# Delta rule and feed-forward on one core: where chunk 1's keys are turned, where w_in's third quarter waits, and how VectorE's background work is listed

## The chip, the cores and the metric

The kernel runs on one core of a Trainium2 chip. The metric is the device time of one execution in microseconds (us). A core has five engines that run beside each other, each in its own order: TensorE (PE; its weight loads are PEld), VectorE (DVE), ScalarE (ACT), GpSimd (POOL) and SyncE (SP), which here only issues DMAs. ScalarE and GpSimd issue some DMAs too. The clock that TensorE is granted changes during a run and is part of the profile.

## The reference

There are 4 batches of 8 heads, 768 positions of width 48. For each head a state matrix is carried along the sequence, and its output goes through a feed-forward block:

```python
k_n = k / (np.linalg.norm(k, axis=-1, keepdims=True) + 1e-06)
for t in range(S):
    y[:, :, t] = einsum('bhd,bhde->bhe', q[:, :, t], state)
    v_old = einsum('bhde,bhd->bhe', state, k_n[:, :, t])
    state = state + beta[t] * outer(k_n[:, :, t], v[:, :, t] - v_old)
x = y.transpose(0, 2, 1, 3).reshape(3072, 384)
h = x @ w_in            # 384 x 2048
out = (h / (1 + exp(-1.702 * h))) @ w_out     # 2048 x 384
```

w_in and w_out come in double precision (two 32-bit words an element), and the kernel turns them into 32-bit floats itself.

## The kernel before

**Units and steps.** The sequence is cut into 6 chunks of 128 positions; a unit is one chunk of one batch with its 8 heads, so there are 24 units, numbered chunk by chunk (units 0 to 3 are chunk 0, 4 to 7 chunk 1). Within a chunk the recurrence becomes a triangular system with the keys' products (gram, line 357, kept as G). It is solved in 4 blocks of 32 rows: `solve` multiplies by the inverse of a diagonal block (psU, copied by ScalarE to US), `below` multiplies the result by the rows underneath (psR), and `rest` subtracts this from V on VectorE. `scores` turns the queries (psT, QS) and makes the masked query-key products (psQ, M, with an affine_select on POOL); `queries`, `outputs` and `state` make psY, copy it to xT and add the new state to ST.

**Inverses.** `invert` (line 427) inverts all diagonal blocks of a chunk (or of two batches) on VectorE: NT holds the blocks, one head and block in a partition, YB the inverse. It is a chain of 25 products P, each with a sum. The blocks reach NT through DRAM (Nd), and the inverses come back through DRAM (Yd) as XB. For chunk 0 `diagonal` (line 411) makes the 32x32 blocks alone on TensorE (psD), copied to TW by VectorE and ScalarE. For all later units `prepare` (line 384) turns the keys (`turn`, psT copied to kT), makes the whole gram, sends all of G to DRAM and reads the blocks from there.

**Raw weights.** `conversion` (line 201) turns raw double words into floats with five VectorE instructions and a ScalarE Relu between them, through a scratch place in TW. w_in is converted in 8 pieces of 3x256 columns (two for each quarter), then w_out in 14 pieces (12 of one row block of 384, two of two). The raw words of w_in lie in the place of w_out, which has room for two quarters: quarters 0 and 1 are fetched at the start, 2 when 0 is converted, 3 when 1 is. w_out's raw words follow by a table, `fetches`: a transfer is issued when a given piece is done. `fill(n)` (line 289) issues the next n conversion instructions, and the program calls it at places written by hand.

**Order of the head.** All engines keep the order in which the program issues (`pinned`), and so does SP's queue of DMAs. The order is: chunk 0's keys are normalised and turned, its blocks made and inverted (`invert(0)`, interleaved with the first scores); then two pairs of units, 0 and 1, then 2 and 3, are solved in 8 hops each (`hops`, line 1031: a hop solves a block for one unit and multiplies below for the other). In the first pair each hop is followed by 4 filler products (`warm(NU)`, ps_warm) and `fill(1)`. After it come the loads of keys 7 and 8, the first raw words of w_out and queries. In the second pair each hop is followed by `fill(2)`, by a half `feed` of the first feed-forward product from hop 3 on, and by the work of `keys()` (line 1044): normalising unit 4 to 7's keys (ScalarE square, VectorE sum, POOL power, VectorE product), turning them, making G and sending the blocks round. `hidden` (line 678) makes the product ph and the activation gT; a half is 3 matmuls, a whole `hidden` 16 halves.

After the pairs the rest of w_in is converted, then `invert(1)` runs, one instruction pair for each of 25 halves of `feed`, and then 10 more conversion instructions (`fill(10)`).

**Woven steps.** From there `woven(n, share)` (line 921) runs for n from 3 to 24. Each step carries the three units n-1, n, n+1, normalises and prepares the keys of unit n+5, and takes `share` us of feed-forward work from a queue by the costs that the work yields (1.3 for a half). The queue begins with `both_written` (line 823), the second product (po) of the first feed-forward block, which goes through w_out's row blocks in the order of conversion and issues conversions (`fill(3)`, and more while the block isn't done) ahead of each; then `written`. Together they fill steps 3 to 6 (share 10.4). From step 7 on (share 19.5) the rest of the feed-forward blocks follow, with one product fewer of each eight (`seven`, for which POOL makes the combinations T1 to T4, L711).

Most instructions go through one helper and so have line 109 in the profile; tiles tell them apart.

Of the kernel before, what the change touches and what calls it, by code (L numbers as in the profile page):

```python
# [18 lines left out]
def kernel(  # L19
# [147 lines left out]

    def quarter(i):
        size = KC * NQ * 2
        return as_raw(raws[:, i % 2 * size : (i % 2 + 1) * size], (KC, NQ))  # L170

    def fetch_in(i, other=None):

        f = slice(i * NQ, (i + 1) * NQ)
        dst = as_rows(quarter(i))
        for j in range(KC):
            for p, r, m, step in x_rows:
                (other if other and p >= DP else sync)(
                    out=dst[p : p + m, j], in_=moe_w_in[r + j * step : r + j * step + m, f]
                )  # L180
# [18 lines left out]
    turns = [0]  # L199

    def conversion(dst, raw, shape):
# [12 lines left out]
        yield  # L214
        turns[0] ^= 1
        at = 3072 + turns[0] * 768
        t = TW[:, at : at + shape[0] * shape[1]].bitcast(I32).rearrange("p (j n) -> p j n", j=shape[0])
        f = t.bitcast(F32)
        ts(t, hi, E1 - 1, E1, op0=AND, op1=OR)
        yield  # L220
        stt(out=f, in0=lo.bitcast(U32), scalar=2.0**-32, in1=t, op0=ALU.mult, op1=ALU.add)
        yield
        stt(out=p, in0=hi, scalar=-(1 << 31), in1=p, op0=AND, op1=OR)
        yield
        stt(out=dst, in0=f, scalar=2.0**-20, in1=dst, op0=ALU.mult, op1=ALU.mult)
        yield

    def pieces():

        for i in range(4):  # L230
            for e in range(2):
                at = i * NQ + e * NPC
                raw = quarter(i)[:, :, e * NPC : (e + 1) * NPC, :]
                yield w_in[:, :, at : at + NPC], raw, (KC, NPC), ("in", 2 * i + e)
# [14 lines left out]
    def conversions():  # L249
# [3 lines left out]
        def begin(i):  # L253
            dst, raw, shape, name = whole[i]
            ops = conversion(dst, places[name[1]] if raw is None else raw, shape)
            next(ops)
            return ops

        after = begin(0)
        yield  # L260
        for i in range(len(whole)):
            ops = after
            next(ops)
            yield
            next(ops)
            yield
            if i + 1 < len(whole):
                after = begin(i + 1)
                yield
            next(ops)  # L270
            yield
            next(ops)
            done.add(whole[i][3])
            fetches.pop(whole[i][3], lambda: None)()
            yield

    fetches = {
        ("in", 1): lambda: fetch_in(2),
        ("in", 3): lambda: fetch_in(3),
        ("in", 5): lambda: fetch_out(3),  # L280
        ("in", 7): lambda: (fetch_out(4), fetch_out(5), fetch_out(6), fetch_out(7)),
# [5 lines left out]
    converting = conversions()  # L287

    def fill(n):
        for _ in range(n):  # L290
            next(converting, None)

    ready = {}
    inverse = {}

# [53 lines left out]

    def transposed(src, dst):  # L350
# [29 lines left out]
    def turn(n):  # L380
        kTs[n] = wk.tile([128, NP, 128], F32, tag="kT", name="kT", bufs=5)
        transposed(KN[n % len(KN)], kTs[n])
# [28 lines left out]
    def diagonal(b, D_):  # L411

        kT = kTs[b]
        ps = [ps_seq.tile([128, NP, 128], F32, tag="seq", name="psD") for _ in range(2)]
# [6 lines left out]
        for e in range(2):  # L421
            for blk in range(NB):
                u = slice(blk * BS, (blk + 1) * BS)
                copy = vec.tensor_copy if e == 0 or blk == 0 else act.copy
                copy(D_[u, e::2, :], ps[e][u, :, u])

    def invert(c, b0=0, nb=B):
# [7 lines left out]
        yield 0.0  # L435
# [20 lines left out]
        for i in range(1, HS):  # L456
# [6 lines left out]
            yield 0.0  # L463
# [3 lines left out]
        act.activation(X1, halves(Y)[1].rearrange("p l i -> p i l"), ACT.Copy)  # L467
        A = N[:, 0:HS, 0:HS]
        N10, Y0 = N[:, HS:, 0:HS], halves(Y)[0]
        for j, Q in ((0, 2), (2, 2), (4, 4), (8, 4), (12, 4)):  # L470
# [7 lines left out]
            yield 0.0  # L478
        for i, Q in ((0, 4), (4, 4), (8, 4), (12, 2), (14, 2)):
# [7 lines left out]
            yield 0.0  # L487
# [21 lines left out]
        yield 0.0  # L509
# [7 lines left out]
    class Step:  # L517
# [114 lines left out]
        def state(self, psS=None):  # L632
# [3 lines left out]
            for h in range(H):  # L636
# [4 lines left out]
                )  # L641
            St = ST[:, self.b, 0 : NP * D].rearrange("p (j d) -> p j d", j=NP)
            vec.tensor_tensor(St, psS, St, op=ALU.add)

        def outputs(self, state=False):
# [5 lines left out]
            if state:  # L651
                self.state(self.psS)
# [20 lines left out]

    def g_tile():

        return wk.tile([128, FQ, NTH], F32, tag="gT", name="gT", bufs=GB)
# [146 lines left out]
    def both_written(c, gT):  # L823

        po = [ps_moe.tile([128, DM], F32, tag="moe", name="po") for _ in range(HB)]
        for n, f in enumerate(order):
            while ("out", f - f % 2 if 4 <= f < 8 else f) not in done:
                fill(1)
            fill(3)
# [151 lines left out]
    for i in range(B, len(KN)):  # L981
        pool.memset(KN[i][:, :, D:DP], 0.0)

# [13 lines left out]
    for b in range(B):  # L997
# [3 lines left out]
        )  # L1001
    for b in range(B):
        load(b, ((QP, q),), sync)
    for b in range(B):
        load_values(b, sync)
    fetch_in(1, other_queue)
    for n in range(B, len(KN)):
        load(n, ((KN, k),), sync)
    for blk in range(NB):
        sync(out=bI[blk::NB, 1:], in_=betas[:, 1:, blk, :])  # L1010
    fill(6)
    for b in range(B):
        gram(b)
        warm(NA)
    late_U = spare("U")[:, 0 : H * D + XR]
    pair = [new_step(n) for n in range(B)]
    inverting = invert(0)
    for n in range(B):
        next(pair[n].scored)
        warm(NA)  # L1020
        run(pair[n].scored)
        warm(NA)
        if n == 0:
            ahead_of(inverting, 18)
    run(inverting)
    pool.memset(late_U[:, H * D :], 0.0)
    for s in pair:
        s.select()
    fill(5)
# [9 lines left out]
    def put_out(s):  # L1039
        s.queries()  # L1040
        s.outputs(True)
        steps.pop(s.n)

    def keys():

        def unit(n):
            yield from normalize_mixed(n)
            yield from prepare(n)

        work = [unit(n) for n in range(B, 2 * B)]  # L1050
        for t in range(18):
            for u in range(B):
                s = t - 3 * u
                if s >= 0 and s % 2 == 0:
                    next(work[u], None)
            yield
        for w in work:
            run(w)

    path = hops(*pair[:2])  # L1060
    for i in range(2 * NB):
        together(*next(path))
        warm(NU)
        fill(1)
    for s in pair[:2]:
        put_out(s)
        fill(1)
    load(7, ((KN, k),), sync)
# [16 lines left out]
    preparing = keys()  # L1085
    for i in range(2 * NB):
        together(*next(path))
        if i > 2:
            feed()
        fill(2)  # L1090
        ahead_of(preparing, 2 if i else 0)
    for s in pair[2:]:
        put_out(s)
        feed()
        fill(2)
        ahead_of(preparing, 2)
# [4 lines left out]
    while not ("in", 7) in done:  # L1101
        fill(1)
    run(preparing)
    inverting = invert(1)
    first = new_step(B)
    for i in range(25):
        ahead_of(inverting, 1)
# [5 lines left out]
    run(inverting)  # L1113
    while ffn:
        feed()
    fill(10)
# [35 lines left out]
```

## Time and profile before

| what | us |
|---|---|
| median of 3 runs (812.78 to 814.7) | 812.81 |
| the profiled execution, whole | 808.59 |
| its span in the profile | 806.6 |
| busy in the span: PE, DVE | 745.0, 499.7 |
| busy in the span: ACT, POOL | 238.6, 251.3 |
| mean granted TensorE clock | 0.951 |

The profile is of one execution, and its rows are timed from the start of its span. A group or timeline row names the engine, the line, the operation, the tile written and the tiles read (out<-in), the shape and the number; a bracket gives the engine's idle time before the row and what ended it. A matmul of 32-bit floats stands as two records. The window rows give busy time of each engine in a stretch, the granted clock (1.00 is full) and the share of the 16 DMA engines. The chain of work that ended last lists, in order of time, the pieces that the end waited for.

### The profile page before, as it was taken

The numbers are of one execution on the slowest core, as the hardware profiler recorded it, in microseconds if no ns is written. First come the engines' busy times: TensorE is split into PE (matmuls) and PEld (weight loads), VectorE is DVE, ScalarE is ACT, GpSimd is POOL, SyncE is SP. The second block draws the span as 40 slices with busy tenths as digits, with TensorE's granted clock in tenths as the row PEclk, the third lists the DMA queues.
The fourth block names the chain that finished last, engine by engine and source line by source line (L and its number), as shares of the span: only waits on it lengthen the run. The fifth ranks groups of instructions, "written<-read, shape, count | busy, mean of one in ns | idle before, by whom it ended". The sixth has DMA issues, their size and how long they took to land.

```text
span 806.6 us, 19689 instructions
## 1 busy us (share of the span) xinstructions
PE 745.0 (92%) x8464; PEld 633.7 (79%) x8464; DVE 499.7 (62%) x1029; ACT 238.6 (30%) x523; POOL 251.3 (31%) x222
## 2 busy tenths in 40 slices
PE   8678779777788899999999999999999999999998
PEld 6566668654455689889898898898898898988988
DVE  5798571898688767767677777786686671110000
ACT  3332353223322332232232332322322312312020
POOL 5002030011126735244262272272260320502213
PEclk9576799889999999999999999999999999999999
DMA  9946366344212420421422223214204011000000
GB/s 164 143 69 118 93 172 167 55 108 106 82 55 51 104 53 21 105 54 34 91 54 69 57 64 93 59 28 104 63 12 103 13 25 39 2 26 2 25 1 20
DMA packets 143655, 54.45 MB, mean 68 GB/s; under 512 B 113665, under 2 KB 138369, under 8 KB 143569
## 3 DMA queue, kind: packets, MB, share of 16 engines
q1 hardware_dynamic: 141936, 48.42, 27.2%
q0 software_dynamic: 1536, 4.52, 2.3%
q8 instruction: 66, 1.08, 0.6%
q10 hardware_dynamic: 96, 0.26, 0.1%
q14 instruction: 21, 0.16, 0.1%
HBM read 33.13 MB, written 18.87 MB: 64 GB/s over the span
## 4 chain that ended last, share of the span: by engine, by line
PE 67%; DVE 15%; issue 5%; DMA 5%; POOL 4%; SPq 2%; ACT 1%; DVEq 0%; POOLq 0%
PE ph L109 25%; PE po L109 23%; PE psY L109 5%; PE psU L109 5%; DVE P L109 4%; PE psQ L109 3%; DVE YB L109 3%; SPq L109 2%; DVE TW L109 2%; PE psR L109 2%; PE psT L109 2%; DVE w_out L109 2%; POOL TW L711 2%; DVE NT L109 1%; PE psG L109 1%
## 5 line engine op out<-in xcount | busy, mean ns | idle before, releaser
L109 PE MATMUL ph<-xT,w_in 128*128 128x256 f32 x1152 | 267.4, 389 | 0.0
L109 PEld LDWEIGHTS ph<-xT,w_in 128*128 128x128 f32 x1152 | 219.0, 194 | 33.0 <-DVE V L109 1.4
L109 PE MATMUL po<-w_out,gT 128*128 128x192 f32 (+1 forms) x736 | 150.3, 357 | 18.5 <-DVE w_out L109 10.8
L109 PEld LDWEIGHTS po<-w_out,gT 128*128 128x128 f32 x736 | 121.3, 191 | 36.6 <-DVE w_out L109 14.8
L711 POOL TENSOR_TENSOR gT<-gT 128x512 f32<-128x512 f32 x80 | 105.9, 1332 | 125.6 <-ACT gT L109 115.0
L109 DVE TENSOR_TENSOR V<-V,psR 64x384 f32<-64x384 f32 (+1 forms) x96 | 53.3, 556 | 130.5 <-PE psR L109 129.3
L109 DVE TENSOR_TENSOR P<-NT,YB 64x2 f32<-64x2 f32 (+9 forms) x200 | 97.3, 486 | 6.4
L109 ACT ACTIVATE gT<-ph 128x512 f32<-128x512 f32 x92 | 54.8, 596 | 152.9 <-PE ph L109 152.8
L109 PEld LDWEIGHTS psU<-V,XB 32*32 32x32 f32 x1536 | 61.7, 110 | 31.3 <-issue 15.4
L109 DVE TENSOR_REDUCE YB<-P 64x2 f32<-64x2 f32 (+9 forms) x200 | 81.7, 409 | 6.9
L109 PE MATMUL po<-TW,gT 128*128 128x192 f32 x480 | 83.0, 328 | 0.0
L109 ACT COPY US<-psU 32x384 f32<-32x384 f32 x92 | 43.2, 469 | 125.0 <-PE psR L109 115.1
L109 PE MATMUL psU<-V,XB 32*32 32x48 f32 x1536 | 73.2, 209 | 6.2 <-DVE V L109 5.3
L109 PEld LDWEIGHTS po<-TW,gT 128*128 128x128 f32 x480 | 77.9, 190 | 1.1 <-issue 0.3
L109 PE MATMUL psR<-US,G 32*32 32x48 f32 x2208 | 64.0, 208 | 0.8 <-ACT US L109 0.5
L578 POOL TENSOR_SCALAR_AFFINE_SELECT M<-M 128x1024 f32<-128x1024 f32 x19 | 23.7, 1245 | 120.0 <-DVE M L109 62.1
L109 DVE TENSOR_TENSOR o<-o,po 128x192 f32<-128x192 f32 x40 | 13.5, 351 | 75.8 <-PE po L109 75.3
L109 PEld LDWEIGHTS psR<-US,G 32*32 32x32 f32 x2208 | 54.2, 109 | 2.4 <-ACT US L109 1.1
L109 DVE TENSOR_TENSOR P<-NT 64x512 f32<-64x512 f32 (+7 forms) x50 | 44.5, 890 | 2.1
L94 POOL DMA_DIRECT2D KN<-in_k_dram x15 | 14.4, 960 | 93.5 <-PE psY L109 93.5
L109 PE MATMUL ps_warm<-ident 128*128 128x256 bf16 x176 | 31.6, 340 | 11.5 <-ACT G L109 6.5
L109 PE MATMUL psQ<-QS,kT 48*128 48x176 f32 (+1 forms) x368 | 35.6, 337 | 4.8 <-ACT QS L109 4.7
(110 smaller groups left out, 773.9 us busy)
## 6 DMA issues: line engine op xcount, KB each, us to landing
Nd<-G SPq DMA_DIRECT2D x20, 512.0 KB, 3.5
V<-in_v_dram SPq DMA_DIRECT2D x24, 192.0 KB, 3.1
out_dram<-o SPq DMA_DIRECT2D x24, 192.0 KB, 2.5
QP<-in_q_dram SPq DMA_DIRECT2D x22, 192.0 KB, 3.3
w_out<-in_moe_w_in_dram SPq DMA_DIRECT2D x18, 192.0 KB, 5.1
raw<-in_moe_w_out_dram SPq DMA_DIRECT2D x9, 384.0 KB, 5.3
NT<-Nd SPq DMA_DIRECT2D x24, 128.0 KB, 2.8
XB<-Yd SPq DMA_DIRECT2D x24, 128.0 KB, 3.1
```

Source lines behind the costliest of these rows:

```text
L94: dma(out=place(dst, n)[:, :, 0:D], in_=src[b, :, c * C : (c + 1) * C, :].rearrange("h p d -> p h d"),)
L109: return lambda *a, **kw: tc.keep_in_program_order(op(*a, **kw))
L578: (pool if self.n < B else nc.gpsimd).affine_select(out=self.M, in_=self.M, compare_op=ALU.is_gt, fill=0.0, base=0, pattern=[[0, H], [1, 1 ...
L711: (engine or nc.gpsimd).tensor_tensor(o, a, b, op=op)
```

## The change

Seven things change, all ahead of or inside the woven steps 3 and 4.

- Chunk 1's four keys are loaded at the start, ahead of the queries. Three go to their ring places; the fourth (unit 7, whose ring place still holds unit 0's key) goes to KX in TW and is copied to the ring by a DMA after the first pair.
- `normalize_second` normalises all four right behind inverse 0, ahead of the masks' selects on POOL. `keys` and `normalize_mixed` are no longer called.
- The first pair's hops carry, in place of the filler products, the turning of a key (even hops) and its diagonal blocks (odd hops, psD in ps_moe's banks, all eight copies on ScalarE, DMA issued by ScalarE). NT's four loads follow the hops on SP. The grams of chunk 1 go to the even hops of the second pair, and G is not sent to DRAM for them.
- w_in's quarter 2 gets a third place for its raw words, three of the six gT tiles, and is fetched at the start; it is converted in 3 pieces of 512. Quarter 3 is fetched when quarter 0 is done. w_out's blocks 4 to 7 are fetched after quarter 1, block 3 after quarter 3.
- The conversion writes the mantissa over the raw words instead of a place in TW, and the order of its instructions changes.
- `background` is one list for VectorE: w_in's conversion, then `invert(1)`, then w_out's conversion. `fill(us)` takes instructions from it until their written costs reach us. It is called after each hop, inside `put_out` between the state's product and its addition, in each of the 25 feed halves, and before each po block.
- In inverse 0 a 16x16 copy moves from ScalarE to VectorE, and all of inverse 0 is issued after the scores (those have no VectorE work).

The core of the diff, with what is only renamed or moved left out:

```diff
     def quarter(i):
         size = KC * NQ * 2
-        return as_raw(raws[:, i % 2 * size : (i % 2 + 1) * size], (KC, NQ))
+        at = 1 if i == 1 else 0
+        return as_raw(raws[:, at * size : (at + 1) * size], (KC, NQ))
...
+        if i == 2:
+            for j in range(KC):
+                words = g_tile().rearrange("p f t -> p (f t)").bitcast(I32)
+                thirds.append(as_raw(words, (1, NQ)))
...
         ts(p, hi, 0x7FF * E1, None, op0=AND)
         act.activation(p, p, ACT.Relu, scale=8.0, bias=low)
-        yield
-        turns[0] ^= 1
-        at = 3072 + turns[0] * 768
-        t = TW[:, at : at + shape[0] * shape[1]].bitcast(I32).rearrange("p (j n) -> p j n", j=shape[0])
-        f = t.bitcast(F32)
-        ts(t, hi, E1 - 1, E1, op0=AND, op1=OR)
-        yield
-        stt(out=f, in0=lo.bitcast(U32), scalar=2.0**-32, in1=t, op0=ALU.mult, op1=ALU.add)
-        yield
+        yield 0.75
         stt(out=p, in0=hi, scalar=-(1 << 31), in1=p, op0=AND, op1=OR)
-        yield
+        yield 0.95
+        ts(hi, hi, E1 - 1, E1, op0=AND, op1=OR)
+        yield 0.7
+        f = lo.bitcast(F32)
+        stt(out=f, in0=lo.bitcast(U32), scalar=2.0**-32, in1=hi, op0=ALU.mult, op1=ALU.add)
+        yield 0.95
         stt(out=dst, in0=f, scalar=2.0**-20, in1=dst, op0=ALU.mult, op1=ALU.mult)
-        yield
+        yield 0.95
...
     fetches = {
-        ("in", 1): lambda: fetch_in(2),
-        ("in", 3): lambda: fetch_in(3),
-        ("in", 5): lambda: fetch_out(3),
-        ("in", 7): lambda: (fetch_out(4), fetch_out(5), fetch_out(6), fetch_out(7)),
+        ("in", 1): lambda: fetch_in(3),
+        ("in", 3): lambda: [fetch_out(f) for f in (4, 5, 6, 7)],
+        ("in", 7): lambda: fetch_out(3),
...
-    def fill(n):
-        for _ in range(n):
-            next(converting, None)
+    def background():
+
+        converting = conversions()
+        while ("in", 7) not in done:
+            yield next(converting)
+        yield from invert(1)
+        done.add("inverse")
+        yield from converting
+
+    behind = background()
+
+    def fill(us):
+        while us > 0:
+            us -= next(behind, us)
...
+    def normalize_second():
+
+        z, r = (TW[:, a : a + B * H].rearrange("p (b h) -> p b h", b=B) for a in (1792, 1856))
+        sq = spare("squares")[:, 0 : 2 * H * D].rearrange("p (o h d) -> p o h d", o=2, h=H)
+        for o in range(0, B, 2):
+            for i in range(2):
+                act.activation(sq[:, i], home(B + o + i)[:, :, 0:D], ACT.Square)
+            vec.tensor_reduce(z[:, o : o + 2], sq, axis=AX.X, op=ALU.add)
+            fill(0.7)
+        for o in range(B):
+            pool.tensor_tensor(r[:, o], z[:, o], half, op=ALU.pow)
+        fill(2.5)
+        vec.tensor_scalar(r, r, 1e-6, None, op0=ALU.add)
+        vec.reciprocal(r, r)
+        for o in range(B):
+            K = home(B + o)[:, :, 0:D]
+            vec.tensor_tensor(K, K, r[:, o].broadcast_to([128, H, D]), op=ALU.mult)
...
-                copy = vec.tensor_copy if e == 0 or blk == 0 else act.copy
+                copy = vec.tensor_copy if shared and (e == 0 or blk == 0) else act.copy
...
     run(inverting)
+    normalize_second()
     pool.memset(late_U[:, H * D :], 0.0)
     for s in pair:
         s.select()
-    fill(5)
+    Dx = TW[:, 3584:4608].rearrange("p (b h j) -> p b h j", b=B, j=BS)
+    Ndx = []
+
+    def send_diagonal(b):
+        diagonal(B + b, Dx[:, b], False)
+        Nd = dram.tile([H * C * BS], F32, tag="Nd", name="Nd", bufs=4)
+        beside(out=Nd.rearrange("(h p k) -> p h k", p=C, k=BS), in_=Dx[:, b])
+        Ndx.append(Nd)
...
     path = hops(*pair[:2])
     for i in range(2 * NB):
         together(*next(path))
-        warm(NU)
-        fill(1)
+        (send_diagonal if i % 2 else turn)(i // 2 if i % 2 else B + i // 2)
+        fill(1.7)
+    for b in range(B):
+        sync(
+            out=NT[b * NB * H : (b + 1) * NB * H].rearrange("d i k -> d (i k)"),
+            in_=Ndx[b].rearrange("(d r) -> d r", r=BS * BS),
+        )
     for s in pair[:2]:
         put_out(s)
-        fill(1)
-    load(7, ((KN, k),), sync)
+    sync(out=KN[0], in_=KX)
     load(8, ((KN, k),), sync)
...
     for i in range(2 * NB):
         together(*next(path))
+        if i % 2 == 0:
+            gram(B + i // 2)
         if i > 2:
             feed()
-        fill(2)
-        ahead_of(preparing, 2 if i else 0)
+        fill(1.7)
...
-    while not ("in", 7) in done:
-        fill(1)
-    run(preparing)
-    inverting = invert(1)
     first = new_step(B)
     for i in range(25):
-        ahead_of(inverting, 1)
+        fill(1.0)
         feed()
...
-    fill(10)
+    while not "inverse" in done:
+        fill(0.1)
+    fill(8)
```

In `both_written` the `fill(3)` before each block becomes `fill(2.5)`.

## The prediction

> **What bounds the kernel now.** I read the page's slices first. TensorE is above 98% busy from about 300 us to the end (the two-step window at 300.7 below), and the change touches no step there, so only the head can gain or lose. Window rows in time order (us, PE, PEld, DVE, ACT, POOL busy, granted clock, DMA share, GB/s) size it:
>
> ```profile
> 127.00:170.00 43.00, 38.22 (x176) 32.52 (x172) 25.54 (x55) 11.04 (x22) 1.09 (x1) 0.92 0.35 83
> 173.65:222.50 48.85, 38.07 (x358) 22.42 (x358) 38.61 (x79) 16.66 (x32) 8.64 (x7) 0.93 0.46 120
> 222.50:266.50 44.00, 38.23 (x558) 25.59 (x556) 37.58 (x78) 13.29 (x33) 20.78 (x18) 0.96 0.20 49
> 300.70:357.80 57.10, 56.41 (x710) 50.29 (x706) 39.90 (x85) 17.56 (x40) 24.03 (x19) 1.00 0.26 63
> ```
>
> The second row is woven steps 3 and 4, with both_written between them: TensorE is idle for 10.8 of 48.85 us. Why, the chain that ended last (start, length, what) tells:
>
> ```profile
> 132.40 7.63 DMA Nd<-G
> 140.05 2.63 DMA NT<-Nd
> 142.70 1.24 DVE NT L109
> ...
> 170.13 1.23 DVE NT L109
> ...
> 186.05 1.56 PE po L109 x4
> ```
>
> The key blocks of chunk 1 come round through DRAM so late that their inversion starts at 142.7; it holds VectorE to 171.4, and only then does VectorE convert w_out, which the po products eat as it appears. The timelines of VectorE and TensorE say the same (the bracket is idle time before, and its releaser):
>
> ```profile
> 102.33 0.69 DVE L109 TENSOR_SCALAR w_in<-w_out 128x768 int32<-128x768 int32 x1 [5.14 <-DMA w_out<-in_moe_w_in_dram]
> 142.70 1.23 DVE L109 TENSOR_TENSOR NT<-NT,bI 128x1024 f32<-128x1024 f32 x1 [15.79 <-DMA NT<-Nd]
> ...
> 173.65 4.51 PE L109 MATMUL po<-w_out,gT 128*128 128x384 f32 x8 [4.12 <-ACT w_out L109]
> ...
> 186.05 1.56 PE L109 MATMUL po<-w_out,gT 128*128 128x384 f32 x4 [2.87 <-DVE w_out L109]
> 201.88 1.56 PE L109 MATMUL po<-w_out,gT 128*128 128x384 f32 x4 [2.46 <-DVE w_out L109]
> 206.90 1.87 PE L109 MATMUL po<-w_out,gT 128*128 128x384 f32 x4 [2.66 <-DVE w_out L109]
> ```
>
> VectorE idles 15.79 us for the blocks and 5.14 us for w_in's third quarter; TensorE later pays with eight waits at po. The change aims at both holes. I follow it in marks on the profiled execution.
>
> **1. Start of the first pair: later.** Up to the end of inverse 0 (58.5) little moves: a 16x16 copy goes from ScalarE to VectorE (+0.4; a 256-element product takes 0.42). The four more key and query loads and the third quarter's 12 transfers go out before 58; the DMA share is 0.46 from 40 to 60, so there is room, and if XB comes late (63 before) it is covered by what follows, which lasts to 69. Behind the inverse stands normalize_second. Squares from 59.4, 0.51 each; a 768-element sum about 0.95 (a 384 one takes 0.55); first sums at 61.5; then four POW on POOL at 1.64 to 2.28: to 68.2. Then 0.16 + 0.20 + one 0.56 multiplication: key 4 is ready at 69.3, the fourth at 71.0. The transposes of key 4 stand in TensorE's queue ahead of hop 1, so hop 1's products, which could run at 64, wait to 70.4. Before VectorE's first subtraction come three conversion instructions (0.94 + 0.69 + 0.96), and the selects of the masks on POOL now run from 68.3 to 74 beside them. Under the same selects at 58.8 to 64.6 five such instructions took 7.06 in place of 4.50: +2.5. First subtraction: 71.0 + 2.6 + 2.5 = 76.1, against 66.32.
>
> **2. Hops of the first pair: longer.** Before, subtractions 1 to 6 run from 66.32 to 78.64, 2.46 a hop. Now an even hop carries four transposes (1.06 at clock 0.50, 0.60 at 1.0) and an odd one 16 psD records (2.13 or 1.16), eight copies of 0.26 and a DMA issue of 0.4 on ScalarE, ahead of the next US copy. Products of a hop take about 1.5 at half clock. Two hops on TensorE: 1.5 + 1.06 + 1.5 + 2.13 = 6.2, about 0.3 for a US copy behind the eight: 6.5, so 3.25 a hop; at full clock VectorE sets it, 0.56 + 1.9 = 2.5. I take 3.2 (clock 0.50 is what 68 to 84 shows). Subtraction 6: 76.1 + 5 x 3.2 = 92.1. From there to the second ST addition it took 7.7 (78.64 to 86.33); 1.7 of filling adds 1: 101, against 86.3. The 32 removed ps_warm products (8 groups of about 0.6 to 1.0) are inside the old 2.46.
>
> The granted clock from 68 to 84 is 0.50 although these groups stood there. The Trainium skill, "TensorE: Matmul & The Clock Gate", section "HAM oscillation — how this bites in real kernels", speaks against dropping them: idle gaps longer than some 3.4 us drop the clock to half, and the wait for key 4 is such a gap. Its other half says that sustained products bring the clock back within one window; then the hops would go at 2.5 and this mark would be 97.5 in place of 101.
>
> **3. Second pair and what gates it.** Each hop does a subtraction (1.14 or 0.56) and about 2.2 of filling on VectorE; TensorE has gram products on even hops (1.16) and a feed half (1.4) from hop 3. The old stalls (5.14 for w_in, 1.64 to 2.28 for each POW) are gone. But SP is in order: NT's four loads wait for the last block, then six xT copies (4.7 before), the copy of KX and a key load, and only then w_out's first raw words, about 7 after the pair's end, 5.3 to land: 113.5. VectorE reaches the instruction that reads them at hop 2, about 110, and the subtraction of hop 3 stands behind it: 3.5 lost (0 to 5). Subtraction 3 at 114.8, three more hops at 3.0: 124; then 2.7 + 2.3 + 2.8 of inversion before the first ST addition, 132, whose xT copies stand behind the inverse's copy on ScalarE, so that two ph banks run full. The free run of feed halves starts at 132.6, against 127.2.
>
> **4. Free run.** 25 halves of 1.4 (x12 records in 2.79) and 3.3 for the first scores: 38.4; the 4.31 wait at 156.8, where ScalarE stood behind the inverse, goes, since the inverse is over by 147 (10.8 after the second addition at 136). First po at 171.0, against 173.65. VectorE by then has converted 46 of 70 instructions (36 x 0.44 + 10 x 0.80 = 24 from 147: 171), so po waits for nothing.
>
> The new conversion has the same five VectorE instructions for an element, the mantissa written over its own words; quarter 2 as three pieces of 512 lies between the 384 rows (0.35 to 0.56) and the 768 rows (0.69 to 0.96), some 9.3 for 9.0. Only two instructions (1.04 at 384) now lie between an exponent and its reader, with ScalarE's 0.62 in between; a gT of 0.60 in its way costs up to 0.3 a piece, 0 to 4 us over w_out. I take none on the path: by then VectorE has the po groups of steps 3 and 4 as cover, and without it the 4 would be paid there. The copy of KX to KN is off the path until step 7 and costs its 0.4 issue.
>
> **5. Steps 3 and 4.** TensorE's own work: 16 po groups at 1.39 = 22.2; psU/psR 4 x 0.87, psT 4 x 0.6, psG 2 x 1.16, psQ 2 x 1.46 = 11; 33 in all. Steps 5 and 6, with as many po products and more hops, need 38.2 and take 44, 5.8 lost to chains. Taking the same 5.5 here: 38.5, against 48.85. VectorE has 10.6 of conversion left in it, no bound.
>
> **Sum.** 171.0 + 38.5 + 584.1 (unchanged from 222.5 to 806.6) = 793.6 span, 13.0 less. Gains: 10.3 in steps 3 and 4, 2.7 before them (first pair 14.7 later, second 9.2 shorter than its 40.8, free run 8.1 shorter than its 46.5). The profiled execution took 808.59 (2.0 outside the span); the runs' median is 812.81, 4.2 more, so I subtract from the median: 800.
>
> **Rivals.**
> A, as summed: 800. Chance 0.45.
> B, the clock comes back in the hops and the raw words land in time: 3.5 + 3.3 more, and steps 3 and 4 lose only 2.5 (35.5, 3 more): 22.8 in all, 790. For it: more 128-wide work in each hop. Against: clock 0.50 with TensorE nearly full at 76 to 84. Chance 0.20.
> C, the waits at po only change their name: steps 3 and 4 are held by the chain of normalisation, gram and subtractions at 44, as 5 and 6 are: 5.5 less gain, 805. For it: at 233, 255 and 282 psT waits 2.8 to 3.0 for POOL's key. Against: no inversion stands before those keys here. Chance 0.20.
> D, slower: TensorE stays at half clock through both pairs. ScalarE's eight copies then come out serial in each odd hop (1.1 more a hop, 7), seven ph halves at 2.93 in place of 1.56 (9.6), four grams (3.8), seven hops (4.2): 24.6 lost, 824. It outweighs the gain from the point where the free run starts after 145.6. For it: clock 0.50 at 92 to 98 and 106 to 108, after idle spells. Against: 1.0 from 112 on before. Chance 0.15.
> That the change misses its end (the inverse still late) I count under D: the blocks are issued by hop 7, NT is read at hop 4 of the next pair, 15 us after.
>
> **Numbers.** Likeliest 800. D's core lies outside; A's own spread is 795 to 806 (first pair 3.5, raw words 3.5, steps 3 and 4 3 each way). Range 789 to 811. About 0.3% (2.4 us) is what a measurement of this kernel can tell from no change: faster beyond it 0.81 (A, B, C less their tails), within 0.06, slower 0.13.
>
> **What would show it.** Step 1: first V subtraction near 76, psT of key 4 near 69.5 after a TensorE gap. Step 2: hops of 3.2, second ST addition near 101, clock 0.5. Step 3: a VectorE wait of about 3.5 for raw, before a w_out conversion near 110. Step 4: no 15.79 wait; NT product of the inverse near 117, its last near 146; po starting near 171 without waits on w_out. Step 5: n=6's scores near 209.5 in place of 222.5; after it every mark shifted alike. Wrong would be: a wait at XB, a NT wait that returns, po waits for raw words still in flight, or a shift that shrinks after step 5.

## The result, and the profile after

The changed kernel takes 801.04 us (median of 4 runs, 797.68 to 803.63), the kernel before 813.75 (4 runs, 812.78 to 817.28): a ratio of 0.9834, 95% interval 0.9801 to 0.9868. Taken again later, six more runs gave 797.07; all ten have a median of 799.5. Of the 48 runs of the kernel before that were timed beside the experiments, six were in a slower state (820 us and more) and count in none of the medians and ratios. The profiled execution of the changed kernel took 803.63 (span 801.4, mean clock 0.94) and lies above its median, that of the kernel before (808.59) below its own, so the two spans differ by only 5.2. The second profile of the same code, called **again** below (798.27, span 796.1), is the better one to lay beside the forecast.

Window rows of the changed kernel (first profile), columns as before: the free run of feed halves, steps 3 and 4, step 5, step 6, and two later steps.

```profile
136.69:172.89 36.20, 36.09 (x180) 31.08 (x177) 32.59 (x59) 14.61 (x30) 2.07 (x2) 1.00 0.49 115
172.89:212.51 39.62, 35.54 (x357) 21.95 (x355) 21.21 (x50) 13.05 (x27) 7.82 (x7) 0.96 0.28 75
212.51:238.90 26.39, 23.41 (x286) 16.06 (x282) 19.02 (x48) 6.93 (x17) 6.24 (x5) 0.81 0.27 70
238.90:261.00 22.10, 19.30 (x280) 12.74 (x278) 18.04 (x30) 6.45 (x16) 14.69 (x13) 0.92 0.14 29
295.54:352.54 57.00, 56.31 (x708) 50.18 (x704) 40.03 (x85) 17.57 (x40) 23.58 (x19) 1.00 0.27 63
```

Steps 3 and 4 fell from 48.85 to 39.62, and TensorE's idle time in them from 10.8 to 4.1. The free run is full (36.09 of 36.20). The late steps are as they were (57.00 for two, 57.10 before).

VectorE's timeline of the changed kernel, the rows that answer to the two holes of before:

```profile
78.03 1.14 DVE L109 TENSOR_TENSOR V<-V,psR 32x384 f32<-32x384 f32 x2
...
94.22 0.42 DVE L109 TENSOR_SCALAR w_in<-gT 128x512 int32<-128x512 int32 x1
...
114.29 0.36 DVE L109 TENSOR_SCALAR w_out<-raw 128x384 int32<-128x384 int32 x1 [4.70 <-DMA raw<-in_moe_w_out_dram]
...
117.01 1.22 DVE L109 TENSOR_TENSOR NT<-NT,bI 128x1024 f32<-128x1024 f32 x1
...
149.05 1.23 DVE L109 TENSOR_TENSOR NT<-YB,bI 128x1024 f32<-128x1024 f32 x1
```

The third quarter (now in gT) is there without a wait, and the inverse's first NT product stands at 117.01 with no bracket, where it had waited 15.79 and begun at 142.70. Its last one ends at 150.3 in place of 171.4. A new wait of 4.70, for w_out's first raw words, has come.

TensorE's timeline of the changed kernel, its longest waits and the first po product:

```profile
72.89 1.08 PE L109 MATMUL psT<-ident,KN 128*128 128x128 f32 x4 [7.01 <-DVE KN L109]
...
172.89 4.34 PE L109 MATMUL po<-w_out,gT 128*128 128x384 f32 x12
...
184.83 0.94 PE L109 MATMUL psT<-ident,KN 128*128 128x128 f32 x4 [4.03 <-POOL KN L330]
...
223.33 1.12 PE L109 MATMUL psT<-ident,KN 128*128 128x128 f32 x4 [2.98 <-POOL KN L330]
```

The po waits on w_out are gone, all eight (seven on VectorE, one on ScalarE). What is left in steps 3 and 4 is one wait of 4.03 for a key. The chain that ended last shows what that key waited for (start, length, what):

```profile
167.34 11.09 issue
178.47 1.71 POOL rn L326
180.18 0.96 POOL ksq L321
181.14 2.77 issue
183.95 0.84 POOL KN L330
184.83 0.94 PE psT L109 x4
```

POOL is held up twice, 11.09 and 2.77, and the engine it waits for is VectorE (for ssq, then for rn), whose list of conversions stood in front. "issue" hides that: the two pieces have no work of their own.

### The profile page after: what moved, and what is told of

Same layout as the page of the kernel before. It is cut to its first block, busy times and chain, and to the rows that moved or that the text cites. A ratio compares the mean times of both kernels' runs of the same rounds, so it can differ in the third digit from the quotient of the medians.

```text
span 801.4 us, 19777 instructions
## 1 busy us (share of the span) xinstructions
PE 747.9 (93%) x8496; PEld 640.4 (80%) x8496; DVE 492.9 (62%) x1027; ACT 246.0 (31%) x555; POOL 248.4 (31%) x223
## 4 chain that ended last, share of the span: by engine, by line
PE 73%; DVE 12%; issue 5%; DMA 4%; ACT 2%; POOL 2%; SPq 1%; ACTq 0%; DVEq 0%; POOLq 0%
PE ph L109 27%; PE po L109 24%; PE psU L109 6%; PE psY L109 5%; DVE P L109 4%; PE psQ L109 3%; DVE YB L109 3%; PE psG L109 2%; PE psT L109 2%; PE psR L109 2%; DVE NT L109 2%; PE psD L109 1%; DMA xT<-last 1%; DMA w_out<-in_moe_w_in_dram 1%; ACT TW L109 1%
## 5 line engine op out<-in xcount | busy, mean ns | idle before, releaser
L109 PE MATMUL po<-w_out,gT 128*128 128x192 f32 (+1 forms) x736 | 147.5, 354 | 3.7 <-DVE o L109 3.6
L109 DVE TENSOR_TENSOR P<-NT,YB 64x2 f32<-64x2 f32 (+9 forms) x200 | 95.2, 476 | 6.4
L109 PEld LDWEIGHTS psU<-V,XB 32*32 32x32 f32 x1536 | 63.6, 111 | 33.5 <-issue 16.1
L109 PE MATMUL psU<-V,XB 32*32 32x48 f32 x1536 | 75.2, 211 | 6.7 <-DVE V L109 5.0
L109 PE MATMUL psR<-US,G 32*32 32x48 f32 x2208 | 65.9, 213 | 0.4 <-ACT US L109 0.4
L109 PEld LDWEIGHTS psR<-US,G 32*32 32x32 f32 x2208 | 56.1, 113 | 2.0 <-ACT kT L109 1.1
L109 PE MATMUL psT<-ident,KN 128*128 128x128 f32 x92 | 18.1, 332 | 23.2 <-POOL KN L330 13.4
L326 POOL TENSOR_TENSOR rn<-ssq,half 128x8 f32<-128x8 f32 x16 | 34.0, 2128 | 11.1 <-DVE ssq L109 11.1
```

Of the source, the lines that this page charges most:

```text
L109: return lambda *a, **kw: tc.keep_in_program_order(op(*a, **kw))
L326: nc.gpsimd.tensor_tensor(rn, ssq, half, op=ALU.pow)
```

## The experiments

**Theory.** The gain comes from w_out's conversion being moved off the po products: the keys turned early let the inverse start 25 us sooner, VectorE then reaches w_out during the free run, and steps 3 and 4 lose their po waits. **Rivals:** it comes from the list alone (no early keys needed), or from the third place; what is left to gain lies in the clock, in POOL's powers, or in the raw words. All edits are to the changed kernel. Medians in us, with the ratio to the kernel before in the same batch of runs (its medians are 814.37, 813.27 and 809.69 for the three batches; the ratio is estimated from the single runs, so it isn't quite the quotient of two medians):

| batch, kernel | median | ratio, 95% interval |
|---|---|---|
| 1 again (unaltered) | 797.07 | 0.9806 [0.9756, 0.9857] |
| 1 late | 805.25 | 0.9889 [0.9853, 0.9925] |
| 1 no_third | 808.16 | 0.9925 [0.9892, 0.9958] |
| 1 keys_late | 805.69 | 0.9911 [0.9879, 0.9943] |
| 2 raw | 795.15 | 0.9758 [0.9715, 0.9801] |
| 2 pow | 800.89 | 0.9822 [0.9777, 0.9867] |
| 2 warm | 800.08 | 0.9832 [0.9790, 0.9874] |
| 2 raw_pow | 796.80 | 0.9773 [0.9732, 0.9815] |
| 3 newton | 795.32 | 0.9794 [0.9752, 0.9836] |
| 3 fill2 | 791.17 | 0.9756 [0.9722, 0.9791] |
| 3 best | 790.30 | 0.9736 [0.9694, 0.9779] |

### again: the same code once more

> The changed kernel once more, with nothing altered. The theory (the list: w_out's conversion now runs ahead of steps 3 and 4, because the inverse of chunk 1 is over by 150) expects a median of 801, 2 either way, po from about 173, and n=6's scores 39 to 40 later. In the profiled execution the stretch from n=6's scores to the end was 588.9 against 584.1 before, 4.4 of it in step 5, where the clock was at 0.50 from 224 to 232. If that belongs to the one execution, this profile has 584 to 585 there and a span near 796; if it belongs to the change, 588 to 589 again.

Its window rows for steps 3 and 4, and for 5 and 6:

```profile
169.30:208.90 39.60, 35.49 (x357) 22.03 (x355) 21.22 (x50) 13.06 (x27) 7.84 (x7) 0.96 0.29 74
208.90:254.50 45.60, 39.82 (x562) 27.08 (x556) 37.16 (x78) 13.36 (x33) 20.80 (x18) 0.93 0.23 55
```

Steps 3 and 4 repeat to 0.02. Steps 5 and 6 do not (48.49 in the first profile, 45.60 here) though no instruction differs: that part is the clock of one execution.

### late: w_out's conversion put back behind the inverse

```diff
     for i in range(25):
-        fill(1.0)
+        if i < 9:
+            fill(1.0)
...
-    fill(8)
```

> VectorE's list stops in the free run of feed halves as soon as the inverse is done, so nearly all of w_out's conversion falls into steps 3 and 4 again, as before the change. The list theory: steps 3 and 4 go back from 39.6 to about 48, waits of TensorE on w_out return at po, the time rises by 8 to 9 to about 810. The rival, that the gain is in earlier transfers or in the clock of the free run: steps 3 and 4 stay near 40 and the time near 801.

TensorE's timeline and the window of steps 3 and 4 in this kernel:

```profile
179.26 1.66 PE L109 MATMUL po<-w_out,gT 128*128 128x384 f32 x4 [2.87 <-DVE w_out L109]
...
196.02 1.56 PE L109 MATMUL po<-w_out,gT 128*128 128x384 f32 x4 [1.71 <-DVE w_out L109]
...
199.94 1.86 PE L109 MATMUL po<-w_out,gT 128*128 128x384 f32 x4 [1.56 <-DVE w_out L109]
```

```profile
168.60:217.10 48.50, 39.72 (x359) 23.29 (x357) 36.05 (x73) 17.38 (x33) 5.97 (x5) 0.89 0.33 86
```

The first po is where it was (168.6), the waits on w_out are back, and steps 3 and 4 take 48.50, the 48.85 of before. So the shorter steps come from w_out being ready. The median rises by 8.2 (5.8 against the median of all ten runs), close to the 8.9 that the two steps lost.

### no_third: without the third place

```diff
-        at = 1 if i == 1 else 0
+        at = i % 2
...
-        ("in", 1): lambda: fetch_in(3),
-        ("in", 3): lambda: [fetch_out(f) for f in (4, 5, 6, 7)],
-        ("in", 7): lambda: fetch_out(3),
+        ("in", 1): lambda: fetch_in(2),
+        ("in", 3): lambda: fetch_in(3),
+        ("in", 5): lambda: fetch_out(3),
+        ("in", 7): lambda: [fetch_out(f) for f in (4, 5, 6, 7)],
```

> w_in's third quarter has no place of its own: it goes to quarter 0's words when that is converted, the fourth to quarter 1's, as before the change, and w_out's blocks 4 to 7 are fetched after the last quarter. All else is the changed kernel. The list theory: quarter 0 is converted by 69, 12 transfers take 7 to issue and 5 to land, 81, and VectorE first reads them at 83: no wait over 1, the time stays at 801, 2 either way. The rival, that the third place carries a part of the gain: the old wait of 5.1 for the third quarter returns and the time is 804 to 807.

It cost 11.1 against **again** in the same batch (8.7 against the median of all ten), so the expectation was wrong. SP's own rows (start, length, transfer) and VectorE's in this kernel:

```profile
70.66 30.31 SPq L109 DMA_DIRECT2D w_out<-in_moe_w_in_dram  x24
...
106.03 5.70 SPq L109 DMA_DIRECT2D NT<-Nd  x4
111.83 3.77 SPq L109 DMA_DIRECT2D xT<-last  x6
...
116.92 1.62 SPq L109 DMA_DIRECT2D raw<-in_moe_w_out_dram  x3
```

```profile
103.01 0.69 DVE L109 TENSOR_SCALAR w_in<-w_out 128x768 int32<-128x768 int32 x1 [5.59 <-DMA w_out<-in_moe_w_in_dram]
...
121.97 0.36 DVE L109 TENSOR_SCALAR w_out<-raw 128x384 int32<-128x384 int32 x1 [10.38 <-DMA raw<-in_moe_w_out_dram]
```

SP's rows in **again**:

```profile
65.81 7.21 SPq L109 DMA_DIRECT2D w_out<-in_moe_w_in_dram  x12
...
85.57 14.74 SPq L109 DMA_DIRECT2D NT<-Nd  x4
101.07 4.37 SPq L109 DMA_DIRECT2D xT<-last  x6
...
107.53 1.52 SPq L109 DMA_DIRECT2D raw<-in_moe_w_out_dram  x3
```

With two places the fourth quarter may not be written until the second is converted. Its 12 transfers sit in SP's queue until about 101, and VectorE waits 5.59 for them inside the first pair, whose second ST addition ends at 111.0 (100.6 in **again**). This profile began late: inverse 0 ends at 63.3 in place of 58.4, so 5.5 of the 10.4 belong to the pair. A wait of the old size (5.14) is thus back, now for the fourth quarter.

The second pair loses another 4.5 to its last ST addition (150.9 in place of 136.0), at the wait for w_out's raw words. They don't come later after the first pair's end than before: the conversion that reads them starts 11.0 after it here and 11.2 in **again**, and in both kernels SP asks for them only behind the xT copies, which start within 1 us of the pair's end. But VectorE stands at that instruction 0.6 after the pair's end in place of 7.3, ahead of the pair's first subtraction and not of its third. The quarter without the third place goes in two pieces in place of three, five instructions fewer in a list that is taken by written cost, so the list is further on. That this alone moved the wait wasn't tried.

The first po then starts 9.0 later than in **again**, counted from inverse 0's end; steps 3 and 4 give 2.3 back (37.28), so up to n=6's scores the marks explain 6.6 of the 8.7 to 11.1. The rest isn't traced.

### keys_late: the list without the early keys

Chunk 1's keys are normalised after the first pair, turned in the even hops of the second pair and sent in the odd ones; the filler products return to the first pair's hops; the list goes on with conversions, some of w_out's among them, until the point of the program where the blocks' loads have been issued.

```diff
-    normalize_second()
...
-        (send_diagonal if i % 2 else turn)(i // 2 if i % 2 else B + i // 2)
+        warm(NU)
...
+    normalize_second()
...
         if i % 2 == 0:
+            turn(B + i // 2)
+        else:
+            send_diagonal(i // 2)
             gram(B + i // 2)
```

> The list without the early keys: chunk 1's keys are normalised after the first pair, turned and their blocks made in the second pair's hops, the first pair has its filler products again, and the inverse stands in the list where its blocks have been sent, with w_out's first pieces ahead of it. The list theory: first pair ends near 88 in place of 102, the inverse runs beside the free run and is over near 165, late by 15 but with four pieces of w_out done ahead of it; steps 3 and 4 then carry some 5 us more of conversion: 799 to 804. The rival, that the early turning of the keys is what pays: back to 808 to 813.

TensorE's and VectorE's rows of this kernel:

```profile
98.53 1.12 PE L109 MATMUL psT<-ident,KN 128*128 128x128 f32 x4 [10.89 <-DVE KN L109]
```

```profile
136.33 1.23 DVE L109 TENSOR_TENSOR NT<-NT,bI 128x1024 f32<-128x1024 f32 x1 [6.83 <-DMA NT<-Nd]
```

The first pair ends at 87.3 rather than 100.6, but the 10.89 and the 6.83 come, the inverse ends only at 164.4, and the first po stands at 177.8, 8.5 later than in **again**. No po waits for w_out even so, and steps 3 and 4 take 38.78: part of w_out is now converted ahead of the late inverse. So the shorter steps come from the list, with or without early keys; what the early keys bring is that the first po starts sooner. They are worth 8.6 in this batch (6.2 against the ten runs), and the time lies between the two expectations.

What the three undone parts cost (8.2, 11.1, 8.6) adds up to more than the whole gain of the batch (17.3), so the costs overlap. The rewritten conversion, the filling inside `put_out` and the moved 16x16 copy were not undone alone.

### raw: w_out's first words ahead of NT's loads

```diff
+    fetch_out(0)
     for b in range(B):
...
-    for f in range(3):
+    for f in range(1, 3):
```

> w_out's first raw words are asked for ahead of NT's loads on SP (their place is free then) and not behind the xT copies. The theory: VectorE's wait for them in the second pair's hop 2 (4.70 and 3.89 in the two profiles of the changed kernel) goes to nothing, with it TensorE's 2.6 at the next hop, and the free run starts 2.5 to 4 earlier: 794 to 797, the changed kernel being at 797 to 801. The rival, that TensorE at half clock sets the second pair anyway: the wait goes and the free run starts where it did, no gain.

VectorE's row at that place in this kernel:

```profile
118.29 0.56 DVE L109 TENSOR_TENSOR V<-V,psR 32x384 f32<-32x384 f32 x1 [3.57 <-PE psR L109]
```

The wait for raw words is gone, and VectorE then waits 3.57 for TensorE a hop later; the first po moves to 167.9 only. The median is 4.9 to 5.7 below the two kernels of the same batch that left the time alone (warm, pow), though its interval still touches theirs. In the profile the marks explain 1.4 of it; the rest isn't traced.

### pow, raw_pow and warm: the start of the first pair

```diff
-        for o in range(B):
-            pool.tensor_tensor(r[:, o], z[:, o], half, op=ALU.pow)
+        pool.tensor_tensor(
+            r, z, half.rearrange("p (o h) -> p o h", o=1).broadcast_to([128, B, H]), op=ALU.pow
+        )
```

> normalize_second's four POW of 8 elements, 6.69 in a row on POOL, become one of 32. It starts after the second sum in place of the first, 1.9 later. If an instruction's price hardly depends on its elements (1.7), key 4 is ready 3 earlier and the first subtraction too: 795 to 798. If it goes with the elements (6.6), it is 1.9 later: 799 to 803. Either way the whole chain behind it should shift by the same amount; a rival is that the first pair is set by something else (the fourth quarter's words, the selects), and then nothing moves.

POOL's rows, the changed kernel's first and this one's second:

```profile
63.49 6.69 POOL L109 TENSOR_TENSOR TW<-TW,half 128x8 f32<-128x8 f32 x4 [2.81 <-DVE TW L109]
```

```profile
64.25 5.51 POOL L109 TENSOR_TENSOR TW<-TW,half 128x32 f32<-128x32 f32 x1 [4.76 <-DVE TW L109]
```

One power of 32 elements takes 5.51, four of 8 took 6.69: the price goes with the elements more than with the instruction. The single one must also wait for the last sums, so it starts 1.9 later after its own wait, and nothing is gained.

> Both edits together: w_out's first raw words asked for early, and one POW of 32. If each shifts the chain where the theory has it, the gains add up: the sum of what the two give alone, 791 to 796. If they hide behind one another, no more than the larger.

The two together gave no more than **raw** alone (796.80).

```diff
+        if i == 0:
+            warm(36)
         (send_diagonal if i % 2 else turn)(i // 2 if i % 2 else B + i // 2)
```

> 36 filler products stand on TensorE ahead of key 4's turning, in the gap of 7 us in which TensorE waits for it. The theory says that the gap lets the clock fall to half, and that the hops then go at 3.05 in place of 2.5, with VectorE waiting 1.2 and 1.6 for TensorE in the last two: with the clock kept the first pair ends 2.5 to 3.5 earlier, 794 to 798. The rival: the hops' small products do not hold the clock (it was 0.50 from 68 to 84 before the change too, behind 28 fillers), so the clock falls inside the hops and the gain is under 1.

Window rows of this kernel:

```profile
60.00:68.00 8.00, 7.23 (x68) 5.78 (x66) 5.86 (x7) 2.49 (x5) 6.61 (x4) 0.93 0.68 148
68.00:76.00 8.00, 4.07 (x84) 3.51 (x84) 7.79 (x10) 1.53 (x3) 4.96 (x6) 0.71 0.88 160
76.00:84.00 8.00, 6.99 (x171) 6.13 (x174) 7.78 (x12) 5.46 (x18) 0.00 (x0) 0.50 0.12 19
84.00:92.00 8.00, 7.62 (x107) 6.28 (x100) 4.75 (x10) 5.38 (x17) 0.00 (x0) 0.50 0.72 217
```

The fillers hold the clock near full to 68, and the hops run at 0.50 all the same; the second ST addition ends at 100.4 (100.6 in **again**). They end at 67.8, and a wait of 3.02 for key 4 is left behind them, so this run does not show hops without any gap ahead of them. The fillers inside the hops, which the change took out, don't hold the clock either: **keys_late** has them, and its clock is 0.50 from 70 to 80.

### newton: the root on VectorE

With the edit of **raw**; the square root of the norms is computed by three Newton steps on VectorE in place of POOL's power.

```diff
-            pool.tensor_tensor(r[:, o], z[:, o], half, op=ALU.pow)
-        fill(2.5)
...
+        ts(y.bitcast(I32), x.bitcast(I32), -0.5, float(0x5F3759DF), op0=ALU.mult, op1=ALU.add)
+        for _ in range(3):
+            stt(out=r, in0=y, scalar=-0.5, in1=y, op0=ALU.mult, op1=ALU.mult)
+            tt(r, r, x, op=ALU.mult)
+            stt(out=y, in0=r, scalar=1.5, in1=y, op0=ALU.add, op1=ALU.mult)
```

> With w_out's first words early (as in raw, 795), normalize_second takes the root on VectorE by three Newton steps, as normalize_first does (14 instructions of 32 elements, 3.3 there), in place of POOL's POW; the filling beside the POW falls away, so four conversion instructions move back in the list. The theory, that the first pair's start is gated by sums, POW and key product: key 4 ready 3 earlier, first subtraction at 72 to 73 in place of 76, free run 3 to 4 earlier, 791 to 793. The rival, that the list of VectorE is what counts: the conversion put off (3.5) is paid behind it in the pairs, and nothing is gained, 794 to 797.

VectorE's first subtraction of the first pair in this kernel:

```profile
70.85 1.14 DVE L109 TENSOR_TENSOR V<-V,psR 32x384 f32<-32x384 f32 x2
```

The first subtraction comes 5 earlier, but the second ST addition ends at 99.2, only 1.0 before **raw**: at a clock of 0.50 from 76 to 96, TensorE is busy for 17.9 of the 20 us and VectorE waits for it (1.36, 1.38, then 3.19). The pair's start was not what its end waited for. The second pair is shorter here (29.0 to its last ST addition, 34.4 in **raw**), but so it is in **raw_pow** (30.5) and **fill2** (30.4), which have POOL's powers; the medians of **newton** and **raw** agree (795.32, 795.15).

### fill2 and best: the list kept out of the key's way

With the edit of **raw**; **best** has that of **newton** as well.

```diff
-    fill(8)
+    fill(2)
```

> With w_out's first words early (as in raw, 795), the last filling before the woven steps is 2 in place of 8. In every profile TensorE waits 4.0 in step 3 for key 8 from POOL, where the prediction had 1. The theory: the sum for key 8 stands on VectorE behind the conversion that fill(8) issues and behind psQ's wait; with some 7 instructions fewer ahead of it (0.45 each) it comes 3 earlier, TensorE's wait falls to 1 to 2, and the time to 792 to 793. The rival: the same conversions are then asked for by both_written in the same step, ahead of the key's second part, and the wait stays.

The reason is in the timeline of **again**, VectorE's rows first and then POOL's:

```profile
174.24 0.55 DVE L109 TENSOR_REDUCE ssq<-ksq 128x8 f32<-128x384 f32 x1
...
179.88 0.17 DVE L109 TENSOR_SCALAR rn<-rn 128x8 f32<-128x8 f32 x1
```

```profile
174.87 1.71 POOL L326 TENSOR_TENSOR rn<-ssq,half 128x8 f32<-128x8 f32 x1 [11.13 <-DVE ssq L109]
176.56 1.00 POOL L321 TENSOR_TENSOR ksq<-KN 128x384 f32<-128x384 f32 x1
180.36 0.83 POOL L330 TENSOR_TENSOR KN<-KN,rn 128x384 f32<-128x384 f32 x1 [2.81 <-DVE rn L109]
```

Key 8's sum (ssq) stands behind the eight microseconds of conversions issued ahead of the woven steps, and after POOL's power (done at 176.6) the small rn addition stands behind more of them until 179.9. TensorE's wait and the window of steps 3 and 4 in **fill2**:

```profile
172.14 0.65 PE L109 MATMUL psT<-ident,KN 128*128 128x128 f32 x4 [0.62 <-POOL KN L330]
```

```profile
163.60:198.20 34.60, 33.93 (x359) 21.21 (x357) 21.27 (x50) 13.01 (x27) 8.24 (x7) 1.00 0.31 84
```

The wait falls from 4.05 to 0.62, though POOL still waits 2.42 for the rn addition; the clock stays at 1.00, and the two steps take 34.60: 5.0 less than in the changed kernel or in **raw** (39.62). (Its first po at 163.6 is another 4.3 ahead of **raw**'s; it is there already at the second pair's last ST addition, 130.3 for 134.6, up to where the two run the same code, so that is no gain of this edit.) Between kernels of one batch, **best** is 5.0 below **newton**, from which it differs in this one line, though their intervals overlap; its steps 3 and 4 take 37.95 where **newton**'s take 41.08. Against **raw**, of another batch, the ratios to the kernel before show nothing (0.9756 for **fill2**, 0.9758 for **raw**). So the shorter steps are shown by the profiles, and what the line is worth in the whole time is not settled.

> Both on top of raw: Newton steps on VectorE, and 2 of filling before the woven steps. If both theories hold, 788 to 791; the sum of what the two give alone against raw.

**best** is the fastest in median, 790.30, 2.6% below the kernel before. The interval of its ratio lies wholly below that of the changed kernel's first four runs, and touches that of **again**; over **fill2** (791.17) it has no gain that shows.

## Why the prediction was right

The forecast was 800, and the ten runs give 799.5. A gain of 13 was forecast; the first runs show 12.7, the later batch 17.3. That steps 3 and 4 shrink because w_out is ready holds by experiment (**late**); that it takes early keys for this does not (**keys_late**). The marks, in us, against both profiles of the changed kernel:

| mark | predicted | first profile | again |
|---|---|---|---|
| inverse 0 ends | 58.5 | 60.4 | 58.4 |
| first V subtraction | 76.1 | 78.0 | 76.0 |
| one hop of the first pair | 3.2 | 3.05 | 3.05 |
| second ST addition ends | 101 | 102.5 | 100.6 |
| wait for w_out's raw words | 3.5 | 4.70 | 3.89 |
| NT product starts, inverse ends | 117, 146 | 117.0, 150.3 | 114.5, 146.7 |
| second ST addition of the second pair | 136 | 139.6 | 136.0 |
| first po | 171.0 | 172.9 | 169.3 |
| steps 3 and 4 | 38.5 | 39.6 | 39.6 |
| scores of n=6 | 209.5 | 212.5 | 208.9 |
| from there to the end | 584.1 | 588.9 | 587.2 |

- **Step 1** held in its end, 76.0 in **again** for 76.1. That the sum fits so well is luck: beside the selects it was the normalisation that took longer (1.11, 0.35 and 1.24 for each of three products, where 0.16, 0.20 and 0.56 had been reckoned), so that key 4's transposes start at 70.9 in place of 69.5, behind a gap of 6.86, and the fourth key is ready at 73.9 in place of 71.0; the three conversions then took 2.1, not the 5.1 that held the allowance for the selects. The first profile is 1.9 late already at inverse 0's end, ahead of all that was priced.
- **Step 2** held: 3.05 a hop for 3.2, at a clock of 0.50. The other side of the clock rule, on which the mark would be 97.5, did not come.
- **Step 3** held in **again**. In the first profile the second pair took 37.1 in place of 35.4 to its second ST addition, with the clock at 0.50 from 120 to 126, where it was 1.00 in **again**.
- **Step 4** was 1.7 too long: from the second addition to the first po the two profiles need 33.3, where 35.0 had been reckoned. No po waits for w_out, as forecast. **late** shows that w_out's conversion ahead of the po products is what takes these waits away. That the inverse has to end early for it, as the forecast had it, is not so: in **keys_late** it ended at 164.4, and no po waited either.
- **Step 5** was right in size (39.6 for 38.5) but for the way it is made up. Only 4.1 of the 5.5 "lost to chains" is there, all in one wait, and TensorE is busy for 35.5 where 33 had been reckoned, at a clock of 0.96. That one wait is rival C's mechanism. Against C stood "no inversion stands before those keys here": true, but the list's conversions stood there instead (**fill2**).
- **Unchanged from 222.5 on: this step failed.** The shift did not stay whole. From the scores of n=6 to the end the profiles of the changed kernel need 588.9 and 587.2, 3.1 to 4.8 more than the 584.1 of before. The code is the same; other kernels with the same code there took 583.8 (**warm**) to 590.7 (**no_third**), so 584.1, from one execution, lay at the light end. In the first profile the excess lies in step 5. It took 26.39 at clock 0.81 (row above). The window row of the kernel before for the same step:

```profile
222.50:244.50 22.00, 19.02 (x284) 12.81 (x282) 19.08 (x48) 6.84 (x17) 6.16 (x5) 1.00 0.26 68
```

  22.00 at clock 1.00, with two instructions fewer on record and 4.4 less of TensorE's busy time: the same products, run faster.
- **The sum.** 793.6 was forecast for the span, 796.1 came in **again**: po -1.7, steps 3 and 4 +1.1, the tail +3.1, together +2.5. The median came out right since the forecast subtracted its gain from the median of the kernel before, 4.2 above the profiled execution. The light tail accounts for most of that 4.2 (argued from the marks; no second profile of the kernel before was taken), so the allowance made up for the tail without having named it. That the two fit so closely is partly luck.
- **The third place** was costed as the 5.14 that VectorE had waited. **no_third** brings a wait of that size back (5.59) and loses 8.7 to 11.1 in all: the second pair pays too, since VectorE stands in front of w_out's raw words sooner. The forecast didn't need this price, since it summed the changed kernel's own marks.
- **The rivals.** B did not come: the clock stayed at 0.50 in the hops, and the raw words were late. C came as one wait of 4.0. D needed a free run that starts after 145.6; it started at 133 to 137, with the clock at 1.00.

## What to carry to other kernels

A list of background work on an in-order engine is as good as its order against the short instructions that others wait for: fill up to the point where the next key's sum is issued, not past it (4.0 us of TensorE here). When a buffer is added or taken away, look beyond the wait that it fills: here it also changed how far the list had come when the next words were needed. And a part of the code that is called unchanged should get the spread that several executions show for it, not one profile's figure.

## What the runs showed of the hardware

**The clock after a short gap.** The same wait of 2.98 for a key was followed by half clock in one execution and by full clock in another. The changed kernel's rows around its wait at 223.33, then the row of before around its wait at 233.28:

```profile
220.00:224.00 4.00, 1.02 (x5) 0.67 (x4) 3.67 (x11) 0.00 (x0) 0.83 (x1) 0.83 0.00 0
224.00:228.00 4.00, 4.00 (x62) 2.32 (x64) 3.01 (x6) 0.60 (x1) 0.00 (x0) 0.50 0.00 0
```

```profile
232.00:236.00 4.00, 2.72 (x76) 1.85 (x76) 3.69 (x11) 0.60 (x1) 0.83 (x1) 1.00 0.00 0
```

The drop cost step 5 about 4.4 (26.39 against 22.00). Behind the same wait (2.98 or 2.99) the four transposes took 1.11 or 1.12 in the first profile, **no_third**, **pow**, **raw_pow** and **newton**, and 0.66 in the kernel before, **again**, **warm**, **fill2** and **best**. The Trainium skill, "TensorE: Matmul & The Clock Gate", section "HAM oscillation — how this bites in real kernels", puts the limit at gaps of some 3.4 us; here the drop followed a bracket of 2.98 or 2.99 in five profiles. Why the executions differ isn't shown.

**Half clock with TensorE nearly full.** In the first pair the clock was 0.50 from 76 to 98 in the first profile, with TensorE busy for 19.9 of 22 us, and neither fillers ahead of it (**warm**) nor fillers inside the hops (**keys_late**) raised it. The same page, in its section "What's actually happening", lets the full clock return after some 3.4 us of sustained work; that doesn't agree with the 14 us from 84 to 98, in which TensorE was busy for 13.6. What in these hops, most of them small 32x32 products, holds the clock down was not tried.
